# Windowed attention and a gated feed-forward in one kernel: products added in pairs on VectorE, q and k features taken at stride 4, three padded weight regions

## The chip, the cores and the metric

One Trainium2 chip, one of its cores. The metric is the time of one execution on the device, in microseconds (us).

## What is computed

One sequence of 2048 rows of width 512, in bf16. `xn` is the row-wise layer norm of `x`. Two branches read it:

```
qkv = xn @ wqkv                      # 32 heads of 16 features
logits[s, w] = q[s] . k[s - 2*w] / 4 # w = 0..7, one such row per head; masked where s - 2*w < 0
o = sum_w softmax(logits)[s, w] * v[s - 2*w]
s = o @ wo
g = silu((gelu(xn @ w_gate) * (xn @ w_up)) @ w_down)   # inner width 1792
out = x + s * g
```

So each query sees 8 keys, two rows apart, and the rest is dense matrix products.

## The kernel before

The sequence is cut into 4 blocks of 512 rows (index j). Everything is held with features on partitions and rows along the free dimension, so `xnT` comes from PE transposes (L355) of normalised tiles.

For each block there are these steps:

- **qkv** (L428): 12 groups of 4 matmuls give q, k and v in 4 chunks of 128 features each. A chunk's stationary operand is 128 neighbouring columns of `wqkv_sb`. For block 0 the groups work on halves of 256 rows, so that they can start on two tiles of `x`. ScalarE (ACT) copies each group out of PSUM (L441, L447, L452). v goes through DRAM (`vT_dram`) and comes back as `v_arr` with the window's shifts laid out on partitions (L494).
- **scores**: for `w2` = 0, 1 and each of 4 chunks VectorE (DVE) multiplies q by four shifted views of k into one product tile `prod` of 128x4x512 (L515). PE then sums over the 16 features of each head with a 0/1 matrix `ind`: 4 chunks times 4 shifts, 16 matmuls with 32 output columns each into one PSUM tile `L` (L528), the four shifts on four column strips. ACT takes the exponential (L540). For block 0 a small DVE instruction multiplies by a mask (L544).
- **normalisation**: PE sums the weights over w (L574), DVE takes the reciprocal (L584, L586), PE spreads it (L592), ACT copies it (L602), DVE multiplies (L612).
- **values**: for each half of the 16 features DVE makes four product tiles `pv` (L625), two feature groups times `w2` = 0, 1, and PE sums them over w with the matrix `fold4`, again 16 matmuls (L639); ACT copies `o` out (L650).
- **feed-forward**: 14 pairs of groups of 4 matmuls, `g` and `u` (L686); ACT takes the gelu (L696); DVE multiplies into `hT` (L703).
- **output**, 4 tiles of 128 rows: `y` (14 matmuls, L740), `s` (4 matmuls, L728), ACT's silu (L751), DVE's product and residual (L754, L761), the store (L765).

The order of instructions on every engine is fixed when the kernel is built. Class `Order` places tasks one after the other on modelled engines with durations such as `PROD = 1.14` and `COL16 = 1.1`; the dense matmuls form one chain on PE in the order qkv(0..3), then feed-forward and output of block 0, 1, 2, 3. Scores and values fill in by readiness and priority. A DVE product tile comes from a ring of 6 buffers (`pr`), the PSUM groups of the main chain from a ring of 4 (`f`), `L`, transposes, sums and spreads from a ring of 2 (`a`), `O` from 1.

The matrices are loaded by DMA. `load_wqkv` brings q, k and v columns in three pieces. ACT's queue issues the loads of `w_gate`, `w_up`, `wo` (four pieces) and `w_down`, each behind a step that it is told to wait for: `wo` behind the last k copy of block 2.

Nine matmuls on zeros of 512 columns (L293) run at the start, while `x` is on its way.

Of the kernel before, what the change touches and what calls it, by code (L numbers as in the profile page):

```python
# [19 lines left out]
TQ = 512  # L20
# [4 lines left out]

MM = 0.216
COL16 = 1.1
TR = 0.28
PROD = 1.14
HMUL = 0.6  # L30
# [99 lines left out]
def kernel(  # L130
# [11 lines left out]
    nc = tc.nc  # L142
    B, S, D = A_x.shape
    DF = B_w_gate.shape[1]
    NC = D // P
# [11 lines left out]
    cpool = pool("cpool", 1)  # L157
# [9 lines left out]
    hpool = pool("hpool", 1)  # L167
# [4 lines left out]
    psa = pool("psa", 2, space=bass.MemoryType.PSUM)  # L172
# [23 lines left out]

    def load_wqkv(i):
        nc.sync.dma_start(
            out=wqkv_sb[:, :, i * D : (i + 1) * D], in_=wqkv_v[:, :, i * D : (i + 1) * D]
        )  # L200

    def load_x(t0, t1):
# [24 lines left out]
    mhalf = cpool.tile([P, TPB], F32, name="mhalf")  # L227
    nc.gpsimd.memset(mhalf[:], -0.5)

    IOFF = 24  # L230
    ind = cpool.tile([P, 56], BF16, name="ind")
    nc.gpsimd.memset(ind[:], 0.0)
    nc.gpsimd.memset(ind[:, IOFF : IOFF + 8], 1.0)
    nc.gpsimd.affine_select(
        out=ind[:, IOFF : IOFF + 8],
        in_=ind[:, IOFF : IOFF + 8],
        pattern=[[-16, 8]],
        compare_op=ALU.is_ge,
        fill=0.0,
        base=0,  # L240
        channel_multiplier=1,
    )
    nc.gpsimd.affine_select(
        out=ind[:, IOFF : IOFF + 8],
        in_=ind[:, IOFF : IOFF + 8],
        pattern=[[16, 8]],
        compare_op=ALU.is_gt,
        fill=0.0,
        base=16,
        channel_multiplier=-1,  # L250
    )
    k_sb = cpool.tile([P, NC, PAD + S], BF16, name="k_sb")
# [35 lines left out]
    rstd = cpool.tile([P, NT, 1], F32, name="rstd")  # L288


    warm_ps = psa.tile([P, TQ], F32, name="warm_ps", tag="a")
    for _ in range(9):
        nc.tensor.matmul(warm_ps[:], lhsT=warm[:, 0:P], rhs=warm[:], start=True, stop=True)  # L293
    order.clock["pe"] = 5.0


# [3 lines left out]
    def layer_norm(j):  # L300
# [49 lines left out]
        def transpose(t, dep, on_act):  # L350
            def fn():
                tiles["tr", t] = psa.tile([P, NC * P], BF16, name="tr_ps", tag="a")
                for c in range(NC):
                    cs = slice(c * P, (c + 1) * P)
                    nc.tensor.transpose(tiles["tr", t][:, cs], tiles["xn", t][:, cs], ident[:])  # L355

            def copy():
                o = xnT[:, :, t * P : (t + 1) * P]
                i = tiles["tr", t][:].rearrange("p (c n) -> p c n", c=NC)
                if on_act:  # L360
                    nc.scalar.activation(out=o, in_=i, func=AF.Copy)
                else:
                    nc.vector.tensor_copy(out=o, in_=i)  # L363
# [48 lines left out]
    def qkv(j):  # L412
# [4 lines left out]
        for lo in range(0, TQ, n):  # L417
            for which in range(3):
                for c in range(0, NC, w):
                    key = (j, which, c, lo)  # L420

                    def mms(key=key, which=which, c=c, lo=lo):
                        ps = psf.tile([P, TQ], F32, name="qkv_ps", tag="f")
                        tiles["qkv", key] = ps
                        for i in range(w):
                            fo = which * NC + c + i
                            for dk in range(NC):
                                nc.tensor.matmul(  # L428
                                    ps[:, i * n : (i + 1) * n],
                                    lhsT=wqkv_sb[:, dk, fo * P : (fo + 1) * P],  # L430
                                    rhs=xnT[:, dk, j * TQ + lo : j * TQ + lo + n],
                                    start=(dk == 0),
                                    stop=(dk == NC - 1),
                                )
# [68 lines left out]
    def scores(j, prio):  # L503
        exps = []
        for w2 in range(2):
            prods = []

            def product(c, w2=w2, prods=prods):
                prod = prpool.tile([P, 4, TQ], BF16, name="prod", tag="pr")
                off = j * TQ + PAD - HALO + 8 * w2  # L510
                base = k_sb[:, c, off : off + TQ]
                kwin = bass.AP(
                    tensor=base.tensor, offset=base.offset, ap=[base.ap[0], [2, 4], [1, TQ]]
                )
                nc.vector.tensor_tensor(  # L515
                    out=prod[:],
                    in0=tiles["q", j][:, c, :].unsqueeze(1).to_broadcast([P, 4, TQ]),
                    in1=kwin,
                    op=ALU.mult,
                )  # L520
                prods.append(prod)

            def reduce(w2=w2, prods=prods):
                L = psa.tile([P, TQ], F32, name="L_ps", tag="a")
                tiles["L", j, w2] = L
                for cc in range(NC):
                    for w4 in range(4):
                        nc.tensor.matmul(  # L528
                            L[32 * w4 : 32 * (w4 + 1), :],
                            lhsT=ind[:, IOFF - 8 * cc : IOFF - 8 * cc + 32],  # L530
                            rhs=prods[cc][:, w4, :],
                            start=(cc == 0),
                            stop=(cc == NC - 1),
                        )

            def expo(w2=w2):
                if w2 == 0:
                    tiles["attn", j] = atpool.tile([P, 2, TQ], BF16, name="attn", tag="attn")
                attn = tiles["attn", j]
                nc.scalar.activation(out=attn[:, w2, :], in_=tiles["L", j, w2][:], func=AF.Exp)  # L540

            def masked(w2=w2):
                a = tiles["attn", j][:, w2, 0:PAD]
                nc.vector.tensor_tensor(out=a, in0=a, in1=mask[:, w2, :], op=ALU.mult)  # L544

            ps = []
            for c in range(NC):
                key = ("S", j, w2)
                ps.append(
                    add(  # L550
                        "dve", PROD, lambda c=c, product=product: product(c),
                        deps=[q_ready[j], k_ready[j], *ps[-1:]], prio=prio,
                        takes=[("pr", (*key, c))], opens=key, closes=key if c == NC - 1 else None,
                        frees=[("q", j)] if w2 == 1 and c == NC - 1 else [],
                    )
                )
            r = add(
                "pe", COL16, reduce, deps=[ps[-1]], prio=-0.5, takes=[("a", ("L", j, w2))],
                frees=[("pr", ("S", j, w2, c)) for c in range(NC)],
            )  # L560
# [48 lines left out]
    def values(j, prio):  # L609
# [10 lines left out]
        for half in range(2):  # L620
            pvs = []

            def product(g, w2, half=half, pvs=pvs):
# [6 lines left out]
                )  # L630
                pvs.append(pv)

            def reduce(half=half, pvs=pvs):
                o_ps = pso.tile([P, 2, TQ], F32, name="O_ps", tag="o")
                tiles["O", j, half] = o_ps
                for gg in range(2):
                    for ww in range(2):
                        for e in range(4):
                            nc.tensor.matmul(  # L639
                                o_ps[32 * e : 32 * (e + 1), gg, :],  # L640
                                lhsT=fold4[:, 0, :],
                                rhs=pvs[2 * gg + ww][:, e, :],
                                start=(ww == 0),
                                stop=(ww == 1),
                            )

            def evacuate(half=half):
                if half == 0:
# [8 lines left out]
            for i in range(4):  # L657
# [6 lines left out]
                        takes=[("pr", (*key, i))], opens=key, closes=key if last else None,  # L664
# [3 lines left out]
                )  # L668
            r = add(
                "pe", COL16, reduce, deps=[ps[-1]], prio=-0.5, takes=[("O", (j, half))],  # L670
                frees=[("pr", (*key, i)) for i in range(4)],
            )
            o_ready[j] = add(
                "act", ACT2, evacuate, deps=[r], prio=-0.6, frees=[("O", (j, half))],
# [208 lines left out]
```

## Time and profile before

| What | Value |
|---|---|
| time, median of 13 runs | 238.61 us (236.61 to 239.58) |
| the profiled execution: its own time | 238.75 us |
| its span, first to last instruction | 237.0 us |
| PE busy | 229.0 us, 97% |
| VectorE busy | 157.8 us, 67% |
| ScalarE busy | 109.8 us, 46% |
| GpSimd busy | 28.1 us, 12% |
| mean granted TensorE clock | 0.997 |

The thirteen times are 236.61, 236.97, 237.07, 237.12, 237.24, 237.25, 238.61, 238.62, 238.73, 238.75, 239.12, 239.33 and 239.58 us: six up to 237.25, seven from 238.61.

A duration in the trace runs from an instruction's start to its end, and neighbours on one engine overlap: what a row of equal instructions costs its engine is read from start to start. A line of the time line gives the start, the length of the merged stretch, and how many instructions are in it. PEld are the weight loads, which run beside the matmuls.

### The profile page before, as it was taken

The numbers are of one execution on the slowest core, as the hardware profiler recorded it, in microseconds if no ns is written. First come the engines' busy times: TensorE is split into PE (matmuls) and PEld (weight loads), VectorE is DVE, ScalarE is ACT, GpSimd is POOL, SyncE is SP. The second block draws the span as 40 slices with busy tenths as digits, with TensorE's granted clock in tenths as the row PEclk, the third lists the DMA queues.
The fourth block names the chain that finished last, engine by engine and source line by source line (L and its number), as shares of the span: only waits on it lengthen the run. The fifth ranks groups of instructions, "written<-read, shape, count | busy, mean of one in ns | idle before, by whom it ended". The sixth has DMA issues, their size and how long they took to land.

```text
span 237.0 us, 3474 instructions
## 1 busy us (share of the span) xinstructions
PE 229.0 (97%) x1334; PEld 106.6 (45%) x1357; DVE 157.8 (67%) x238; ACT 109.8 (46%) x166; POOL 28.1 (12%) x68
## 2 busy tenths in 40 slices
PE   7899999999999999999999999999999999999992
PEld 2696553443443443434444444444444444444441
DVE  4789998899999999999999321334332243433232
ACT  3466567475766345855532332463342244334211
POOL 7102920300333120003000000000000000000000
PEclk9999999999999999999999999999999999999998
DMA  6993799598497680007200001000000110000011
GB/s 185 358 364 118 159 209 366 141 296 282 130 192 163 126 183 0 22 26 178 46 0 3 0 0 44 22 25 0 1 3 0 44 44 0 3 0 1 22 35 32
DMA packets 15073, 22.66 MB, mean 96 GB/s; under 512 B 1472, under 2 KB 11984, under 8 KB 15056
## 3 DMA queue, kind: packets, MB, share of 16 engines
q0 software_dynamic: 2592, 8.54, 16.4%
q1 hardware_dynamic: 8592, 7.57, 10.2%
q10 hardware_dynamic: 3872, 6.32, 7.8%
q8 instruction: 10, 0.16, 0.3%
q14 instruction: 7, 0.06, 0.1%
HBM read 18.22 MB, written 4.21 MB: 95 GB/s over the span
## 4 chain that ended last, share of the span: by engine, by line
PE 83%; DMA 8%; DVE 6%; issue 1%; ACT 0%; ACTq 0%; DVEq 0%
PE g_ps L686 21%; PE y_ps L740 20%; PE u_ps L686 20%; PE qkv_ps L428 9%; DMA wu_sb<-in_B_w_up_dram 7%; PE s_ps L728 6%; PE O_ps L639 3%; DVE prod L515 3%; PE L_ps L528 2%; PE tr_ps L355 1%; DMA x_sb<-in_A_x_dram 1%; DVE rs L584 1%; DVE stats L307 1%; PE b_ps L592 0%; DVE sg L754 0%
## 5 line engine op out<-in xcount | busy, mean ns | idle before, releaser
L703 DVE TENSOR_TENSOR hT<-gl,u_ps 128x512 bf16<-128x512 bf16 x56 | 38.1, 683 | 33.5 <-PE u_ps L686 29.5
L696 ACT ACTIVATE gl<-g_ps 128x512 bf16<-128x512 f32 x56 | 33.2, 597 | 52.2 <-PE g_ps L686 47.7
L686 PE MATMUL g_ps<-xnT,wg_sb 128*128 128x512 bf16 x221 | 57.0, 379 | 0.2
L686 PE MATMUL u_ps<-xnT,wu_sb 128*128 128x512 bf16 x216 | 56.6, 379 | 0.4
L740 PE MATMUL y_ps<-wd_sb,hT 128*128 128x512 bf16 x218 | 50.7, 379 | 0.4
L428 PE MATMUL qkv_ps<-xnT,wqkv_sb 128*128 128x512 bf16 (+1 forms) x235 | 45.7, 345 | 0.9 <-DVE xnT L363 0.6
L515 DVE TENSOR_TENSOR prod<-q_sb,k_sb 128x2048 bf16<-128x2048 bf16 x32 | 37.7, 1218 | 1.0 <-PE L_ps L528 1.0
L625 DVE TENSOR_TENSOR pv<-attn,v_arr 128x2048 bf16<-128x2048 bf16 x32 | 37.9, 1216 | 0.0
L686 PEld LDWEIGHTS <-wg_sb 128*128 128x128 bf16 x224 | 21.7, 98 | 27.2 <-issue 1.6
L754 DVE TENSOR_TENSOR sg<-sil,s_ps 128x512 bf16<-128x512 bf16 (+2 forms) x17 | 11.1, 653 | 34.2 <-PE s_ps L728 22.9
L686 PEld LDWEIGHTS <-wu_sb 128*128 128x128 bf16 x224 | 21.5, 98 | 27.4 <-issue 2.1
L740 PEld LDWEIGHTS <-hT 128*128 128x128 bf16 x224 | 21.6, 98 | 26.1 <-issue 0.4
L428 PEld LDWEIGHTS <-wqkv_sb 128*128 128x128 bf16 x240 | 23.2, 101 | 18.5 <-issue 1.7
L751 ACT ACTIVATE sil<-y_ps 128x512 bf16<-128x512 f32 x16 | 9.6, 597 | 41.2 <-PE y_ps L740 41.2
L494 POOL DMA_DIRECT2D v_arr<-vT_dram x32 | 18.6, 589 | 65.5 <-DVE pv L625 50.3
L728 PE MATMUL s_ps<-wo_sb,o_sb 128*128 128x512 bf16 (+2 forms) x67 | 16.2, 366 | 0.0
L441 ACT ACTIVATE q_sb<-qkv_ps 128x512 bf16<-128x512 f32 x16 | 9.5, 601 | 6.0 <-PE qkv_ps L428 6.0
L307 DVE BATCH_NORM_STATS2 stats<-x_sb 128x6 f32<-128x512 bf16 x16 | 10.8, 672 | 2.0 <-DMA x_sb<-in_A_x_dram 2.0
L447 ACT ACTIVATE k_sb<-qkv_ps 128x512 bf16<-128x512 f32 x16 | 9.4, 597 | 5.2 <-PE qkv_ps L428 5.2
L452 ACT ACTIVATE vst<-qkv_ps 128x512 bf16<-128x512 f32 x16 | 9.2, 600 | 4.6 <-PE qkv_ps L428 4.6
L728 PEld LDWEIGHTS <-o_sb 128*128 128x128 bf16 x68 | 6.5, 98 | 7.3
L650 ACT ACTIVATE o_sb<-O_ps 128x1024 bf16<-128x1024 f32 x8 | 8.2, 1022 | 1.9 <-PE O_ps L639 1.4
(55 smaller groups left out, 113.9 us busy)
## 6 DMA issues: line engine op xcount, KB each, us to landing
v_arr<-vT_dram POOLq DMA_DIRECT2D x32, 260.0 KB, 5.2
vT_dram<-vst SPq DMA_DIRECT2D x16, 128.0 KB, 5.0
out_dram<-sg SPq DMA_DIRECT2D x15, 128.0 KB, 1.7
wg_sb<-in_B_w_gate_dram ACTq DMA_DIRECT2D x1, 1792.0 KB, 7.4
wu_sb<-in_B_w_up_dram ACTq DMA_DIRECT2D x1, 1792.0 KB, 15.7
wd_sb<-in_B_w_down_dram ACTq DMA_DIRECT2D x1, 1792.0 KB, 9.2
wqkv_sb<-in_A_wqkv_dram SPq DMA_DIRECT2D x3, 512.0 KB, 6.4
x_sb<-in_A_x_dram SPq DMA_DIRECT2D x2, 512.0 KB, 8.9
```

The costliest lines, as they stand in the source:

```text
L307: nc.vector.bn_stats(out=stats[:, t, :], in_=x_sb[:, t, :])
L428: nc.tensor.matmul(ps[:, i * n : (i + 1) * n], lhsT=wqkv_sb[:, dk, fo * P : (fo + 1) * P], rhs=xnT[:, dk, j * TQ + lo : j * TQ + lo + n], ...
L494: nc.gpsimd.dma_start(out=v_arr[32 * w4 : 32 * (w4 + 1), :, :], in_=src)
L515: nc.vector.tensor_tensor(out=prod[:], in0=tiles["q", j][:, c, :].unsqueeze(1).to_broadcast([P, 4, TQ]), in1=kwin, op=ALU.mult,)
L625: nc.vector.tensor_tensor(out=pv[:], in0=tiles["attn", j][:, w2, :].unsqueeze(1).to_broadcast([P, 4, TQ]), in1=tiles["va", j, half][:, 4 * ...
L686: nc.tensor.matmul(ps[:], lhsT=w[:, dk, fc * P : (fc + 1) * P], rhs=xnT[:, dk, j * TQ : (j + 1) * TQ], start=(dk == 0), stop=(dk == NC - 1),)
L696: nc.scalar.activation(out=tiles["gl", j, fc][:], in_=tiles["g_ps", j, fc][:], func=AF.Gelu_apprx_tanh)
L703: nc.vector.tensor_tensor(out=tiles["h", j][:, fc, :], in0=tiles["gl", j, fc][:], in1=tiles["u_ps", j, fc][:], op=ALU.mult,)
L728: nc.tensor.matmul(tiles["s", t][:, cs], lhsT=tiles["o", j][:, c, tt * P : (tt + 1) * P], rhs=wo_sb[:, c, cs], start=(c == 0), stop=(c == ...
L740: nc.tensor.matmul(tiles["y", t][:], lhsT=tiles["h", j][:, fc, tt * P : (tt + 1) * P], rhs=wd_sb[:, fc, :], start=(fc == 0), stop=(fc == N ...
L751: nc.scalar.activation(out=tiles["sil", t][:], in_=tiles["y", t][:], func=AF.Silu)
L754: nc.vector.tensor_tensor(out=tiles["sg", t][:, cs], in0=tiles["sil", t][:, cs], in1=tiles["s", t][:, cs], op=ALU.mult,)
```

## The change

Four things are changed together.

1. **Pairs.** After every second product tile DVE adds the two in place: for the scores chunks 0 and 1, then 2 and 3; for the values `w2` = 0 and 1 of one feature group, that is w and w + 4. PE then sums two tiles instead of four, with 8 matmuls instead of 16 (L and O alike). The second tile of a pair is free again after the addition.
2. **Features at stride 4.** So that chunks can be added before the sum over a head's features, chunk c of q and k now holds the features with d mod 4 = c: the stationary operand takes 128 columns at a step of 4 (from column c of the region). v is unchanged. The 0/1 matrix becomes `quad`: output column h sums partitions 4h to 4h + 3.
3. **Weight regions.** `wqkv_sb` is now three regions, q, k and v, each of 4 x 512 columns and 64 columns of padding. The three loads write the same bytes.
4. **Warm-up.** The PSUM tile of the nine zero matmuls comes from `O`'s pool, and two and three more of 256 columns follow the transposes of tile 0 and tile 1.

The planner's table gets `COL8 = 0.65` for the short sums; an addition is planned at `PROD`.

```diff
-                            lhsT=ind[:, IOFF - 8 * cc : IOFF - 8 * cc + 32],
-                            rhs=prods[cc][:, w4, :],
-                            start=(cc == 0),
-                            stop=(cc == NC - 1),
+                            lhsT=quad[:],
+                            rhs=prods[2 * i][:, w4, :],
+                            start=(i == 0),
+                            stop=(i == 1),
...
+            def pair(i, prods=prods):
+                a, b = prods[2 * i], prods[2 * i + 1]
+                nc.vector.tensor_tensor(out=a[:], in0=a[:], in1=b[:], op=ALU.add)
...
                 for gg in range(2):
-                    for ww in range(2):
-                        for e in range(4):
...
+                    for e in range(4):
+                        nc.tensor.matmul(
+                            o_ps[32 * e : 32 * (e + 1), gg, :],
+                            lhsT=fold4[:, 0, :],
+                            rhs=pvs[2 * gg][:, e, :],
+                            start=True,
+                            stop=True,
+                        )
...
+                                if which < 2:
+                                    ws = slice(dk * D + c + i, (dk + 1) * D, NC)
+                                else:
+                                    ws = slice(dk * D + (c + i) * P, dk * D + (c + i + 1) * P)
                                 nc.tensor.matmul(
                                     ps[:, i * n : (i + 1) * n],
-                                    lhsT=wqkv_sb[:, dk, fo * P : (fo + 1) * P],
+                                    lhsT=wqkv_sb[:, which, ws],
...
-    wqkv_sb = hpool.tile([P, NC, 3 * D], BF16, name="wqkv_sb", tag="h")
+    wqkv_sb = hpool.tile([P, 3, NC * D + 64], BF16, name="wqkv_sb", tag="h")
...
+                if t < 2:
+                    warm_up(2 + t, TQ // 2)
```

Since the planner places all tasks anew, other instructions move too. On VectorE, the stretch before the first value products, before (L515 are the score products, L612 the normalisation; `q_sb_426` is q of block 1, `q_sb_574` of block 2):

```order
L515 TENSOR_TENSOR prod_725<-q_sb_426,k_sb_142 128x2048
L515 TENSOR_TENSOR prod_748<-q_sb_426,k_sb_142 128x2048
L584 RECIPROCAL rs_770<-sum_ps_752 128x128
L586 CAST rs16_772<-rs_770 128x128
L515 TENSOR_TENSOR prod_786<-q_sb_426,k_sb_142 128x2048
L515 TENSOR_TENSOR prod_800<-q_sb_426,k_sb_142 128x2048
L515 TENSOR_TENSOR prod_810<-q_sb_574,k_sb_142 128x2048
L612 TENSOR_TENSOR attn_650<-attn_650,b_sb_802 128x1024
L515 TENSOR_TENSOR prod_837<-q_sb_574,k_sb_142 128x2048
L515 TENSOR_TENSOR prod_846<-q_sb_574,k_sb_142 128x2048
L584 RECIPROCAL rs_863<-sum_ps_848 128x128
L586 CAST rs16_865<-rs_863 128x128
```

and now (L517 are the score products, L527 the additions, L626 the normalisation; `q_sb_430` is q of block 1):

```order
L517 TENSOR_TENSOR prod_694<-q_sb_430,k_sb_141 128x2048
L517 TENSOR_TENSOR prod_715<-q_sb_430,k_sb_141 128x2048
L550 TENSOR_TENSOR attn_648<-attn_648,mask_158 128x16
L527 TENSOR_TENSOR prod_694<-prod_694,prod_715 128x2048
L598 RECIPROCAL rs_748<-sum_ps_730 128x128
L600 CAST rs16_750<-rs_748 128x128
L517 TENSOR_TENSOR prod_759<-q_sb_430,k_sb_141 128x2048
L517 TENSOR_TENSOR prod_773<-q_sb_430,k_sb_141 128x2048
L527 TENSOR_TENSOR prod_759<-prod_759,prod_773 128x2048
L626 TENSOR_TENSOR attn_648<-attn_648,b_sb_780 128x1024
L639 TENSOR_TENSOR pv_806<-attn_648,v_arr_475 128x2048
L639 TENSOR_TENSOR pv_816<-attn_648,v_arr_475 128x2048
```

Before, the scores of block 1 and half of those of block 2 stood ahead of the first value products: 20 score products and 6 value products come before the first `hT`. Now it is half of block 1's scores, 12 and 4 products and 8 additions, and one reciprocal in place of two; the rest stands behind, among the `hT`. On PE this makes 3 sums into `L` ahead of the first `g` instead of 5.

On ScalarE, while block 2's k and v are copied out, before (L447 copies k, L452 copies v, L540 is the exponential, of block 0 for `attn_650`):

```order
L447 ACTIVATE k_sb_142<-qkv_ps_661 128x512
L820 DMA wo_sb_109<-in_A_wo_dram 32x4x512 x4
L540 ACTIVATE attn_650<-L_ps_677 128x512
L452 ACTIVATE vst_720<-qkv_ps_670 128x512
L452 ACTIVATE vst_723<-qkv_ps_698 128x512
L452 ACTIVATE vst_745<-qkv_ps_706 128x512
L452 ACTIVATE vst_750<-qkv_ps_715 128x512
L540 ACTIVATE attn_767<-L_ps_727 128x512
L441 ACTIVATE q_sb_779<-qkv_ps_762 128x512
```

and now (L449, L454 and L546 in the same roles, `attn_648` of block 0):

```order
L449 ACTIVATE k_sb_141<-qkv_ps_656 128x512
L844 DMA wo_sb_109<-in_A_wo_dram 32x4x512 x4
L454 ACTIVATE vst_696<-qkv_ps_665 128x512
L454 ACTIVATE vst_707<-qkv_ps_672 128x512
L546 ACTIVATE attn_648<-L_ps_698 128x512
L454 ACTIVATE vst_724<-qkv_ps_680 128x512
L454 ACTIVATE vst_728<-qkv_ps_688 128x512
L443 ACTIVATE q_sb_745<-qkv_ps_710 128x512
```

The second exponential has moved behind two copies of v, and the third is gone from this place. On PE, 7 groups of qkv (the last three of k and four of v) now stand between the first and the second sum into `L`, where it was 4, and the next block's first q comes right behind the second sum.

More of the change, by code (lines that the diff above doesn't have):

```diff
@@ L243 @@
     nc.gpsimd.affine_select(
[L244 to L249, printed above, removed]
+        out=quad[:], in_=quad[:], pattern=[[4, 32]], compare_op=ALU.is_gt, fill=0.0, base=4,
         channel_multiplier=-1,
@@ L288, with warm_up @@
     rstd = cpool.tile([P, NT, 1], F32, name="rstd")
-    warm_ps = psa.tile([P, TQ], F32, name="warm_ps", tag="a")
-    for _ in range(9):
-        nc.tensor.matmul(warm_ps[:], lhsT=warm[:, 0:P], rhs=warm[:], start=True, stop=True)
+    warm_ps = pso.tile([P, 2, TQ], F32, name="warm_ps", tag="o")
+    def warm_up(count, n):
+        for _ in range(count):
+            nc.tensor.matmul(
+                warm_ps[:, 0, 0:n], lhsT=warm[:, 0:P], rhs=warm[:, 0:n], start=True, stop=True
+            )
+    warm_up(9, TQ)
     order.clock["pe"] = 5.0
@@ L525, in reduce @@
                 tiles["L", j, w2] = L
[L526 removed]
+                for i in range(2):
                     for w4 in range(4):
@@ L668, in values @@
                 )
+                if i % 2 == 1:
+                    ps.append(
+                        add(
+                            "dve", PROD, lambda i=i, pair=pair: pair(i // 2), deps=[ps[-1]], prio=prio,
+                            opens=key, closes=key if last else None, frees=[("pr", (*key, i))],
+                        )
+                    )
             r = add(
-                "pe", COL16, reduce, deps=[ps[-1]], prio=-0.5, takes=[("O", (j, half))],
-                frees=[("pr", (*key, i)) for i in range(4)],
+                "pe", COL8, reduce, deps=[ps[-1]], prio=-0.5, takes=[("O", (j, half))],
+                frees=[("pr", (*key, i)) for i in (0, 2)],
             )
```

50 lines of the change are left out of this document (25 added, 25 removed).

## The prediction

> **What bounds the kernel now.** I read the page's span and engine totals first, then the waits, then the windows of 60 to 130 us and behind it.
>
> ```profile
> span 237.0 us, 3474 instructions
> ...
> PE 229.0 (97%) x1334; PEld 106.6 (45%) x1357; DVE 157.8 (67%) x238; ACT 109.8 (46%) x166; POOL 28.1 (12%) x68
> ```
>
> ```profile
> PE qkv_ps L428 <- DVE xnT L363: 0.6, 1, 0.6
> ...
> PE b_ps L592 <- DVE rs L586: 0.3, 1, 0.3
> ```
>
> ```profile
> 60.00:130.00 70.00, 69.51 (x445) 29.31 (x453) 69.61 (x81) 39.88 (x52) 11.55 (x20) 1.00 0.40 88
> 130.00:237.00 107.00, 102.18 (x482) 46.41 (x489) 36.14 (x59) 34.52 (x51) 0.00 (x0) 0.99 0.05 15
> ```
>
> PE is busy nearly all the time, and once the real work has begun it waits twice for DVE, 0.9 us in all. So PE's queue sets the end. But DVE (the third pair in a window's row) is a second full engine up to 130 us: 69.61 of 70 us. Behind that it needs 36.14 of 107 us. So a microsecond off PE counts if DVE keeps up; and what DVE is given must spread into that later slack without PE reaching a result before DVE has made it.
>
> **Part 1, the shorter sums.** From start to start on PE:
>
> ```profile
> 37.05 1.05 PE L528 MATMUL L_ps<-prod,ind 128*32 128x512 bf16 x16
> 38.03 3.63 PE L428 MATMUL qkv_ps<-xnT,wqkv_sb 128*128 128x512 bf16 x15
> 41.59 1.05 PE L528 MATMUL L_ps<-prod,ind 128*32 128x512 bf16 x16
> ...
> 46.14 0.29 PE L574 MATMUL sum_ps<-attn,fold 128*32 128x128 bf16 x8
> 46.36 2.76 PE L428 MATMUL qkv_ps<-xnT,wqkv_sb 128*128 128x512 bf16 x11
> ```
>
> ```profile
> 108.02 1.05 PE L639 MATMUL O_ps<-pv,fold 128*32 128x512 bf16 x16
> 109.00 0.40 PE L592 MATMUL b_ps<-rs,spread 128*128 128x128 bf16 x4
> 109.23 1.03 PE L728 MATMUL s_ps<-wo_sb,o_sb 128*128 128x512 bf16 x4
> 110.09 0.81 PE L686 MATMUL g_ps<-xnT,wg_sb 128*128 128x512 bf16 x3
> ```
>
> Four full matmuls take 110.09 - 109.23 = 0.86 us, 0.216 each. A sum of 16 takes 0.98 us (38.03 - 37.05), and the 16 matmuls behind it 3.56 (one record is missing in the row) instead of 3.45: 1.09 in all. Sixteen strip matmuls, four abreast, are worth 16 x 0.216 / 4 = 0.86; the other 0.23 goes with the change of shape and stays. Halving takes 0.43 off each sum. There are 8 sums into L and 8 into O: 16 x 0.43 = **6.9 us less on PE**. Were the whole 0.98 in proportion, it would be 7.8: the upper end.
>
> **Part 2, the additions.**
>
> ```profile
> L515 DVE TENSOR_TENSOR prod<-q_sb,k_sb 128x2048 bf16<-128x2048 bf16 x32 | 37.7, 1218 | 1.0 <-PE L_ps L528 1.0
> ...
> L761 DVE TENSOR_TENSOR sg<-sg,x_sb 128x512 bf16<-128x512 bf16 x15 | 6.4, 425 | 0.5
> ```
>
> ```profile
> 59.78 4.62 DVE L625 TENSOR_TENSOR pv<-attn,v_arr 128x2048 bf16<-128x2048 bf16 x4
> 64.32 0.68 DVE L703 TENSOR_TENSOR hT<-gl,u_ps 128x512 bf16<-128x512 bf16 x1
> 64.92 1.22 DVE L625 TENSOR_TENSOR pv<-attn,v_arr 128x2048 bf16<-128x2048 bf16 x1
> ...
> 93.73 0.95 DVE L584 RECIPROCAL rs<-sum_ps 128x128 f32<-128x128 f32 x1
> ...
> 94.86 2.35 DVE L515 TENSOR_TENSOR prod<-q_sb,k_sb 128x2048 bf16<-128x2048 bf16 x2
> 97.13 0.68 DVE L754 TENSOR_TENSOR sg<-sil,s_ps 128x512 bf16<-128x512 bf16 x1
> 97.84 0.43 DVE L761 TENSOR_TENSOR sg<-sg,x_sb 128x512 bf16<-128x512 bf16 x1
> 98.18 0.68 DVE L612 TENSOR_TENSOR attn<-attn,b_sb 128x1024 bf16<-128x1024 bf16 x1
> 98.78 2.35 DVE L515 TENSOR_TENSOR prod<-q_sb,k_sb 128x2048 bf16<-128x2048 bf16 x2
> ```
>
> The residual (L761) is an in-place addition of bf16 tiles, 425 ns for 512 elements; a product takes 1218 for 2048. One line of 0.52 ns an element runs through both, so I give the addition, of the product's shape and kinds, the product's price. In a row that is (64.32 - 59.78) / 4 = 1.14 us. An instruction that reads what the one before it wrote starts after that one's end (L761 at 97.84, L754 ends at 97.81), while an independent one starts 0.09 before it (98.18 against 98.27): 0.12 more, 1.26 us. Thirty-two additions are **40 us more on DVE**, and they cost time only where PE comes to wait.
>
> Whether it does is a balance per block. DVE has now 16 products (18.2), 8 additions (10.1), 14 hT at 64.92 - 64.32 = 0.60 (8.4), four outputs at 98.18 - 97.13 = 1.05 (4.2), reciprocal and cast at 94.86 - 93.73 (1.13) and normalisation (0.60): 42.6 us. PE has 28 groups of 0.86 (24.2), 72 output matmuls (15.5), 4 sums of 0.43 + 0.23 (2.6), and sum over w and spread (0.6): 42.9 us. **The two are level**, and stay so through blocks 0, 1 and 2; only behind the last scores, at some 165 us, does DVE get slack. So it matters where DVE stands when the first block's feed-forward begins.
>
> ```profile
> 26.21 1.21 DVE L515 TENSOR_TENSOR prod<-q_sb,k_sb 128x2048 bf16<-128x2048 bf16 x1
> ...
> 45.48 0.17 DVE L544 TENSOR_TENSOR attn<-attn,mask 128x16 bf16<-128x16 bf16 x1 [0.99 <-ACT attn L540]
> ```
>
> ```profile
> 61.28 1.03 PE L686 MATMUL u_ps<-xnT,wu_sb 128*128 128x512 bf16 x4
> ```
>
> Before, 26 products, two reciprocals and 2.0 us of waits (the mask's 0.99, L515's 1.0 above) lie between 26.21 and the first hT at 64.32. Now it is 16 products, 8 additions and one reciprocal: 64.32 - 10 x 1.14 + 8 x 1.14 + 6 x 0.12 - 1.13 - 2.0 = 59.6. PE's first u ended at 61.28 + 0.86; five long sums ahead of it become three short ones (-5.5 + 2.0), one sum over w, one spread and the 0.3 of waiting go (-0.8): 57.8. DVE starts the first hT 1.8 us behind, and ends it 2.5 behind. Four PSUM banks let PE run three groups, 2.6 us, past a u whose hT is missing: just enough, with no margin. But PE is late for another reason:
>
> **Part 3, what the new order brings.**
>
> ```profile
> 28.50 15.71 DMA wu_sb<-in_B_w_up_dram
> ...
> 44.23 0.57 ACTq L820
> ...
> 44.85 0.61 ACT attn L540
> ```
>
> The last of wo's four loads is issued only when w_up has landed (28.50 + 15.71 = 44.21), and holds ACT's queue until 44.85. Queued behind it are now two copies of v ahead of the second exponential. PE leaves the first L at 37.05 + 0.54, does 28 matmuls (6.15) and the second L (0.54) by 44.3, with all four banks full of v. The next q needs a bank, and the first copy ends at 44.85 + 0.6. **PE waits 1.1 us** (0 if the loads go out sooner, 2 if PE comes sooner and w_up does not). The mask, behind copies and exponential, runs near 46.5. By DVE's own sum it would be 46.1 (45.48, less 2.0 of waits, 12 products become 10 and 4 additions): DVE loses 0.4 where PE loses 1.1, so the first hT is 1.1 instead of 1.8 behind, and there is a margin. I add 0.3 for small waits.
>
> **Part 4, strides and regions.** The weight loads now:
>
> ```profile
> L428 PEld LDWEIGHTS <-wqkv_sb 128*128 128x128 bf16 x240 | 23.2, 101 | 18.5 <-issue 1.7 <-DMA wqkv_sb<-in_A_wqkv_dram 0.8
> ```
>
> The b_ps row above has four loads and their matmuls in 0.23 us, so a contiguous load occupies at most 0.06, behind matmuls of 0.11 (256 columns, part 5) or 0.216. No row shows a strided load. At twice the price it is still hidden, so I take 0; the bounds are 0 and the +8.7 of rival 5. The three loads carry the same bytes: 0.
>
> [...]
>
> **Part 5, warm-up.**
>
> ```profile
> 1.25 4.02 PE L293 MATMUL warm_ps<-warm 128*128 128x512 bf16 x9 [1.25 <-DVE eps_sb L221]
> 5.41 1.13 PE L355 MATMUL tr_ps<-ident,xn_t 128*128 128x128 bf16 x8
> 7.14 4.32 PE L428 MATMUL qkv_ps<-xnT,wqkv_sb 128*128 128x256 bf16 x24 [0.61 <-DVE xnT L363]
> ...
> 12.62 2.78 PE L428 MATMUL qkv_ps<-xnT,wqkv_sb 128*128 128x256 bf16 x24
> ```
>
> ```profile
> 9.86 0.16 DVE L320 RECIPROCAL rstd<-rstd 128x1 f32<-128x1 f32 x1 [0.75 <-ACT rstd L314]
> ...
> 12.82 0.42 DVE L363 COPY xnT<-tr_ps 128x512 bf16<-128x512 bf16 x1 [0.74 <-PE tr_ps L355]
> ```
>
> The first 24 qkv matmuls took 4.32 us, the same 24 later 2.78: PE ran slowly at first, at half speed to go by the nine zero matmuls (4.02 / 9 = 0.45 against 0.216). If the five extra matmuls fill the hole between 5.3 and 7.1 so that PE is at full speed when qkv starts, 1.5 us go. DVE can follow: it stood 0.75 and 0.74 us in that stretch, behind these very matmuls. If they fail, the two between the transposes delay tile 1's by 0.3. The thirteen times of before lie in two groups some 1.7 us apart, and the profiled run is in the upper one: so the slow start may come and go already.
>
> The Trainium skill's "TensorE: Matmul & The Clock Gate" (Part 1) has a gate that opens after a free-running window of 3.4 us in which PE was busy. By it 4.0 us of zeros suffice only by luck, and a longer busy stretch more often.
>
> **The sum**, on the profiled execution's 238.75 us (1.75 above its span, 0.14 above the median of the 13): 238.75 - 6.9 + 1.1 + 0.3 = 233.25. With the warm-up at work 1.5 less, and 0.3 back because w_up need not land as much sooner as PE arrives: **232.0**. Without it, 0.3 more: 233.5.
>
> **The rivals.**
>
> ```profile
> L703 DVE TENSOR_TENSOR hT<-gl,u_ps 128x512 bf16<-128x512 bf16 x56 | 38.1, 683 | 33.5 <-PE u_ps L686 29.5 <-PE g_ps L686 2.1 <-ACT gl L696 1.8
> ```
>
> 1. *Forecast*: shorter sums and full speed from the start, 232.0. Chance 0.44.
> 2. *The slow start remains*: 233.5. For it: the hole is mostly transposes, and five short matmuls may not be enough. 0.33.
> 3. *DVE sets the pace.* If an addition takes 0.1 us more than a product, the 28 ahead of block 3's values put DVE 2.8 us behind, and 42.6 against 42.9 leaves no margin: 235 to 236. For it: two level engines, each now and then waiting for the other. Against: the residual shows no surcharge. 0.11.
> 4. *Additions at hT's rate* (683 ns for 512 where the residual takes 425, 1.03 us more for 2048): 28 x 1.03 = 29 us behind, 261, slower. It decides from a surcharge of 6.6 / 28 = 0.24 us on, where the gain on the median is gone. Against: L761 is all-bf16 in SBUF, as the additions are; hT reads PSUM. 0.04.
> 5. *Strided loads four times as long*, 0.23 us: 64 at 256 columns stick out by 0.115 (7.4), 96 at 512 by 0.014 (1.3): 240.7. 0.04.
> 6. *No gain*, as the sums are not on the path after all: 238.6. Against: PE's 0.9 us of waits. 0.04.
>
> **The numbers.** The likeliest case gives the time. The range takes in cases 1 and 2 and the nearer half of 3: from 229.8 (232.0 less part 1's further 0.9 and part 3's 1.1 plus 0.3, rounded) to 235.6. Left out are 4, 5, 6 and half of 3: 0.18. About 0.5%, 1.2 us, is what a measurement of this kernel can tell from no change. Faster (1 to 3): 0.88; the same (6): 0.04; slower (4 and 5): 0.08.
>
> **What would show it.** In the changed profile: PE busy near 222 us; a sum of 8 in 0.55 us from start to start; additions of 1.22 us; DVE full up to some 165 us, then nearly empty; a wait of PE for a bank near 45 us of about 1 us; q and k weight loads near 101 ns; the first 24 qkv matmuls in 2.8 us (case 1) or 4.3 (case 2). I am wrong if PE waits for hT or for the sums' inputs again and again between 60 and 165 us, if additions last over 1.3 us, or if the first 24 qkv are fast and the time is still above 233.5.

## The result and the profile after

The changed kernel takes 230.9 us in the median of 11 runs (230.51 to 232.31). A twelfth execution on record took 231.96 us; with it the median would be 231.06. The kernel before takes 238.61 in the median of 48 (236.29 to 240.49), the thirteen above included. The ratio is 0.9707, with a 95% interval from 0.9678 to 0.9735. The profiled execution took 232.29 us, with a span of 230.6, and so is one of the slower ones of the eleven: six of them took 230.51 to 230.9. Four executions of the kernels below, of 304.1, 471.57, 471.97 and 823.08 us, lasted far longer than all others of the same kernel (in the two profiled ones, 471.57 and 471.97, PE was at half speed from end to end, and the first 24 qkv matmuls took 5.60 and 5.72 us); with one of 234.5 us in experiment 3, 1.6% above the fastest of its kernel, they are left out of every number that follows.

The page's span, engine totals and DVE's row of the time line (40 slices, busy share in tenths):

```profile
span 230.6 us, 3251 instructions
...
PE 220.4 (96%) x1213; PEld 104.9 (45%) x1234; DVE 193.4 (84%) x270; ACT 111.1 (48%) x167; POOL 27.9 (12%) x67
...
DVE  4799999899999999999999999999849997333222
```

PE has lost 8.6 us of work and DVE has got 35.6 more. DVE is full up to slice 29, some 167 us, once more for three slices behind 173 (block 3's values), and needs a third or less of the last six. The windows ahead of and behind the last scores (PE first, DVE third) say it in microseconds:

```profile
60.00:166.00 106.00, 105.16 (x557) 45.40 (x565) 104.64 (x123) 50.18 (x70) 10.73 (x19) 1.00 0.27 61
166.00:230.60 64.60, 59.66 (x302) 26.75 (x300) 35.13 (x50) 23.75 (x33) 0.00 (x0) 1.00 0.05 17
```

For 106 us both engines run without a gap worth the name: two full engines side by side, where before it was so up to 130 us. Now the groups of the sums and of the additions, and the list of PE's waits (total, times, longest, in us):

```profile
L649 DVE TENSOR_TENSOR pv<-pv 128x2048 bf16<-128x2048 bf16 x16 | 19.5, 1219 | 0.2
L527 DVE TENSOR_TENSOR prod<-prod 128x2048 bf16<-128x2048 bf16 x16 | 19.5, 1219 | 0.2
L534 PE MATMUL L_ps<-prod,quad 128*32 128x512 bf16 x64 | 4.9, 384 | 0.0
L656 PE MATMUL O_ps<-pv,fold 128*32 128x512 bf16 x64 | 4.9, 384 | 0.0
```

```profile
PE qkv_ps L430 <- ACT vst L454: 1.7, 1, 1.7
PE warm_ps L285 <- DVE eps_sb L223: 1.2, 1, 1.2
PE qkv_ps L430 <- DVE mv L304: 1.0, 1, 1.0
```

An addition lasts 1219 ns, as long as a product. The list has no wait of PE for a sum's input, a reciprocal or `hT`; once the real work has begun, what PE waits for is one copy of v. That place on PE's time line (start, length, count; in brackets the idle time ahead) and on ACT's, where ACTq rows are the issuing of DMAs:

```profile
36.44 0.61 PE L534 MATMUL L_ps<-prod,quad 128*32 128x512 bf16 x8
36.99 6.24 PE L430 MATMUL qkv_ps<-xnT,wqkv_sb 128*128 128x512 bf16 x27
43.15 0.62 PE L534 MATMUL L_ps<-prod,quad 128*32 128x512 bf16 x8
45.43 1.89 PE L430 MATMUL qkv_ps<-xnT,wqkv_sb 128*128 128x512 bf16 x8 [1.67 <-ACT vst L454]
```

```profile
40.50 4.16 ACTq L844 DMA_DIRECT2D wo_sb<-in_A_wo_dram  x3
44.78 1.09 ACT L454 ACTIVATE vst<-qkv_ps 128x512 bf16<-128x512 f32 x2 [4.26 <-DMA wu_sb<-in_B_w_up_dram]
```

A sum of 8 takes 36.99 - 36.44 = 0.55 us from start to start, where one of 16 took 0.98. Three issues of `wo` hold ACT's queue for 4.16 us, since the last of them goes out only at 44.09, when `w_up` has landed (27.89 + 16.18 = 44.07; in the trace the two loads share one completion semaphore); the copies of v behind them free the banks, and PE stands 1.67 us. At the start of the program:

```profile
8.04 2.81 PE L430 MATMUL qkv_ps<-xnT,wqkv_sb 128*128 128x256 bf16 x24 [0.98 <-DVE mv L304]
```

```profile
8.03 1.02 PEld L430 LDWEIGHTS <-wqkv_sb 128*128 128x128 bf16 x10 [1.26 <-DMA wqkv_sb<-in_A_wqkv_dram]
```

The first 24 qkv matmuls take 2.81 us instead of 4.32, but start at 8.04 instead of 7.14. The list of PE's waits names DVE's `mv`, which had long been done; the weight loads' row shows the true cause, the q weights, which landed late in this execution.

The two spans differ by 6.4 us. From the rows: 16 sums at 0.98 - 0.55 = 0.43 are 6.9 less; the first qkv matmuls 1.5 less; their later start 0.9 more; the bank wait 1.67 more; the 0.3 that PE waited for a reciprocal is gone. That is 6.1 less, and 0.3 us are left over.

### The profile page after: what moved, and what is told of

The parts are those of the page before. It is cut to its first block, busy times and chain, and to the rows that moved or that the text cites. A ratio compares the mean times of both kernels' runs of the same rounds, so it can differ in the third digit from the quotient of the medians.

```text
span 230.6 us, 3251 instructions
## 1 busy us (share of the span) xinstructions
PE 220.4 (96%) x1213; PEld 104.9 (45%) x1234; DVE 193.4 (84%) x270; ACT 111.1 (48%) x167; POOL 27.9 (12%) x67
## 4 chain that ended last, share of the span: by engine, by line
PE 87%; DMA 8%; DVE 2%; issue 1%; ACT 1%; ACTq 0%; DVEq 0%
PE u_ps L710 21%; PE g_ps L710 21%; PE y_ps L764 21%; PE qkv_ps L430 12%; DMA wu_sb<-in_B_w_up_dram 7%; PE s_ps L752 6%; PE O_ps L656 2%; PE L_ps L534 1%; PE tr_ps L351 1%; DMA x_sb<-in_A_x_dram 1%; DVE stats L303 1%; ACT vst L454 1%; PE sum_ps L588 0%; PE b_ps L606 0%; DVE sg L778 0%
## 5 line engine op out<-in xcount | busy, mean ns | idle before, releaser
L430 PE MATMUL qkv_ps<-xnT,wqkv_sb 128*128 128x512 bf16 (+1 forms) x235 | 43.5, 336 | 2.9 <-ACT vst L454 1.7
L639 DVE TENSOR_TENSOR pv<-attn,v_arr 128x2048 bf16<-128x2048 bf16 x32 | 38.4, 1218 | 0.1
L517 DVE TENSOR_TENSOR prod<-q_sb,k_sb 128x2048 bf16<-128x2048 bf16 x32 | 38.3, 1216 | 0.0
L430 PEld LDWEIGHTS <-wqkv_sb 128*128 128x128 bf16 x240 | 24.9, 108 | 18.0 <-issue 2.5
L649 DVE TENSOR_TENSOR pv<-pv 128x2048 bf16<-128x2048 bf16 x16 | 19.5, 1219 | 0.2
L527 DVE TENSOR_TENSOR prod<-prod 128x2048 bf16<-128x2048 bf16 x16 | 19.5, 1219 | 0.2
L454 ACT ACTIVATE vst<-qkv_ps 128x512 bf16<-128x512 f32 x16 | 9.4, 600 | 7.5 <-DMA wu_sb<-in_B_w_up_dram 4.3
L449 ACT ACTIVATE k_sb<-qkv_ps 128x512 bf16<-128x512 f32 x16 | 9.2, 597 | 3.9 <-PE qkv_ps L430 3.9
```

The lines of the kernel that those rows point to most:

```text
L430: nc.tensor.matmul(ps[:, i * n : (i + 1) * n], lhsT=wqkv_sb[:, which, ws], rhs=xnT[:, dk, j * TQ + lo : j * TQ + lo + n], start=(dk == 0), ...
L517: nc.vector.tensor_tensor(out=prod[:], in0=tiles["q", j][:, c, :].unsqueeze(1).to_broadcast([P, 4, TQ]), in1=kwin, op=ALU.mult,)
L527: nc.vector.tensor_tensor(out=a[:], in0=a[:], in1=b[:], op=ALU.add)
L639: nc.vector.tensor_tensor(out=pv[:], in0=tiles["attn", j][:, w2, :].unsqueeze(1).to_broadcast([P, 4, TQ]), in1=tiles["va", j, half][:, 4 * ...
L649: nc.vector.tensor_tensor(out=a[:], in0=a[:], in1=b[:], op=ALU.add)
```

## The experiments

**1. The sums alone.** The additions stay, but each added tile is read twice, so that PE has its 16 matmuls back (the sum over O in the same way):

```diff
-                for i in range(2):
+                for i in range(4):
...
-                            rhs=prods[2 * i][:, w4, :],
+                            rhs=prods[2 * (i // 2)][:, w4, :],
...
-                            stop=(i == 1),
+                            stop=(i == 3),
...
```

> The changed kernel, but each sum into L and into O is again 16 matmuls, with every added tile read twice (so the sums are doubled, and the output is not the reference's). The additions and the order on VectorE and ScalarE stay. If the sums lie on the path at the size of part 1, PE gets 16 x 0.43 = 6.9 us back: 237.8 us. If their whole length is in proportion, 7.8: 238.7. If PE had hidden room behind VectorE, so that the gain came from something else (the new order, the warm-up), less than 2 us: below 233.

Measured: 237.26 us in the median of 12 runs (236.82 to 238.12), 6.4 above the changed kernel. The groups of the sums, and PE's place of the bank wait:

```profile
L657 PE MATMUL O_ps<-pv,fold 128*32 128x512 bf16 x128 | 8.4, 382 | 0.0
L534 PE MATMUL L_ps<-prod,quad 128*32 128x512 bf16 x128 | 8.4, 382 | 0.0
```

```profile
36.66 1.05 PE L534 MATMUL L_ps<-prod,quad 128*32 128x512 bf16 x16
37.63 6.23 PE L430 MATMUL qkv_ps<-xnT,wqkv_sb 128*128 128x512 bf16 x27
43.80 1.05 PE L534 MATMUL L_ps<-prod,quad 128*32 128x512 bf16 x16
44.80 1.68 PE L430 MATMUL qkv_ps<-xnT,wqkv_sb 128*128 128x512 bf16 x7
```

Both groups are back at 8.4 from 4.9, 7.0 us in all, and the sum is back at 37.63 - 36.66 = 0.97. The wait for a bank is gone, since PE comes later to it; that is why the time rises by less than the 7.0, to 237.26 and not to the expected 237.8. The shorter sums are the bulk of the gain, at the forecast size, and the rival "no gain" is refuted.

**2. The warm-up alone.** The kernel before, with nothing but the five short zero matmuls and the other PSUM tile for them:

```diff
+                if t < 2:
+                    warm_up(2 + t, TQ // 2)
```

> The kernel before with only the warm-up of the change (the zero matmuls' PSUM tile from O's pool, two and three short ones behind the first two transposes). If they bring PE to full speed: 24 matmuls in 2.8 us, the upper group of before's times vanishes, median 236.8 to 237.4 against 238.6, so some 1.5 us of the 7.7 gained come from here and some 6.2 from the rest. If not: 238.6, two groups as before.

Measured: 237.34 us in the median, 236.83 to 238.23 in 11 runs; ratio to the kernel before 0.9938 (0.9908 to 0.9967), 1.5 us. The upper one of the two groups of times is gone. In its profile:

```profile
1.25 4.02 PE L295 MATMUL warm_ps<-warm 128*128 128x512 bf16 x9 [1.25 <-DVE eps_sb L221]
...
7.69 2.79 PE L436 MATMUL qkv_ps<-xnT,wqkv_sb 128*128 128x256 bf16 x24 [0.47 <-DMA wqkv_sb<-in_A_wqkv_dram]
```

The same nine zeros in the same 4.02 us as before, and then 24 matmuls in 2.79 instead of 4.32. Experiment 1's 6.4 and this 1.5 make 7.9, where the whole change gained 7.7: beside the bank wait, nothing of size is left for the new order or the padded regions. The regions were not tried alone.

**3. Everything but the warm-up**, twice:

```diff
-                if t < 2:
-                    warm_up(2 + t, TQ // 2)
```

> The changed kernel without the five short zero matmuls behind the first transposes (the nine long ones stay). If these five bring PE to full speed before the first qkv matmul: the first 24 of 256 columns take about 4.3 us again instead of 2.8, or do so in part of the executions, and the median rises from 230.9 by 0.8 to 1.6 us, to 231.7 to 232.5. If the fast start in the changed kernel's profile was chance: within 0.4 us of 230.9.

> The changed kernel without the five short zero matmuls, once more, for a profile of an execution in which PE is not slow throughout. If the five matmuls are what lets PE start at full speed, the first 24 qkv matmuls take about 4.3 us and the time is 1.3 to 1.8 above the changed kernel's 230.9, some 232.5; if the nine zero matmuls are enough by themselves, 2.8 us and 230.9.

Measured: 230.8, 231.56, 232.55 and 233.84 us in a first series of runs, 230.82, 231.05, 232.22 and 233.19 us in a second. The median of the eight, 231.89, is 1.0 above 230.9. The profile of the second series is of its 230.82:

```profile
1.25 4.02 PE L285 MATMUL warm_ps<-warm 128*128 128x512 bf16 x9 [1.25 <-DVE eps_sb L223]
5.76 0.99 PE L351 MATMUL tr_ps<-ident,xn_t 128*128 128x128 bf16 x8 [0.49 <-DVE xn_t L335]
7.36 2.78 PE L428 MATMUL qkv_ps<-xnT,wqkv_sb 128*128 128x256 bf16 x24 [0.61 <-DVE xnT L359]
```

Here PE was at full speed at 7.36 without any help, after the same 4.02 us of zeros after which it was slow in the kernel before. The clock records kept in the traces (from when on which share of the TensorE clock was granted; ahead of the first record the pages print full speed) say the same: full speed is granted from 6.24 us on here, and from 10.32 us in the kernel before, where the first qkv weight loads start 0.213 us apart up to 10.30 and 0.109 us apart from there on. In the nine profiles with the five extra matmuls it is granted between 3.94 and 6.82 us, each time ahead of the first qkv matmul. So the nine zeros suffice in some executions and not in others. With the five extra matmuls the times end at 232.31 (17 runs of the changed kernel, the six of experiment 5 included); without them three of eight are above that. So the warm-up appears to buy its 1.5 us in a part of the executions; the slower executions without it have no profile, so that they began at half speed is not shown. The profile of the second series gives the second of the two answers that stood in its expectation, and its slower times fit the first: there is no one time without the warm-up.

**4. Stride 4 undone.** q and k take neighbouring columns again, from the padded regions; the features are then not those that the sums need, so the output is not the reference's, and the work is the same:

```diff
-                                if which < 2:
-                                    ws = slice(dk * D + c + i, (dk + 1) * D, NC)
-                                else:
-                                    ws = slice(dk * D + (c + i) * P, dk * D + (c + i + 1) * P)
+                                ws = slice(dk * D + (c + i) * P, dk * D + (c + i + 1) * P)
```

> The changed kernel with q's and k's stationary operands taken from 128 neighbouring columns again, so that the pairs add products of other heads' features and the output is not the reference's; all else as in the changed kernel. If the stride costs nothing, as forecast: weight loads back from 113 to 98 ns at the median, time within 0.3 us of 230.9. If the longer loads reach the path (64 of them stand before matmuls of 256 columns): 0.5 to 1 us faster, 229.9 to 230.4, with the first 24 qkv matmuls below 2.8 us.

Measured: 230.96 us in the median of 6 (230.34 to 232.19), no difference. The 240 weight loads of the changed kernel, two thirds of which are those of q and k, and then of this one (minimum, median and maximum in ns, first and last start):

```profile
L430 PEld LDWEIGHTS <-wqkv_sb x240: 96/113/133, 8.0 to 56.6; 128*128 128x128 bf16 x120
```

```profile
L427 PEld LDWEIGHTS <-wqkv_sb x240: 95/98/99, 7.7 to 55.2; 128*128 128x128 bf16 x120
```

With stride 4 the median load lasts 113 ns, without it 98, and the time does not show it: the loads lie beside matmuls of 0.11 and 0.216 us.

**5. The bank wait taken away.** The fourth issue of `wo`, the one that stood until `w_up` had landed, goes to GpSimd's queue; the compute instructions keep their order:

```diff
-            start(wo_sb[32 * e : 32 * (e + 1), :, :], v[e], k_ready[2])
+            start(
+                wo_sb[32 * e : 32 * (e + 1), :, :], v[e], k_ready[2],
+                nc.gpsimd if e == 3 else nc.scalar,
+            )
```

> The changed kernel with the fourth of wo's loads issued by GpSimd's queue, so that ScalarE's queue is not held until w_up has landed; order of all compute instructions unchanged. If PE's wait of 1.7 us for a PSUM bank near 45 us is on the path: the wait goes, and 1.0 to 1.6 us with it, 229.3 to 229.9. If DVE is next in line (level with PE per block, and some 2 us behind it at the first hT): waits of PE for hT or sums of 0.5 us and more appear between 55 and 165 us, and at most 0.5 us is gained, 230.4 or more.

> The changed kernel as it is, beside the two that follow, so that they are compared on one chip: 230.9 us again, with PE's wait for a PSUM bank near 45 us between 0.7 and 1.7 us in the profile.

> The changed kernel with the issue of wo's fourth load moved from ScalarE's queue to GpSimd's, once more. If the bank wait near 45 us (0.7 to 1.7 us in three profiles) is on the path, 0.5 to 1.0 us below the changed kernel's time of this call; if the first run's 230.4 against 230.9 came from another chip or hour, no difference.

Measured: 230.37 us in the median of 6 (230.3 to 230.81) in the first series; in the second 230.67 (230.27 to 232.81) beside 230.99 (230.47 to 231.8) of the changed kernel itself. The first q behind the second sum on PE, and ACT, in the profile of the first series:

```profile
43.05 1.92 PE L430 MATMUL qkv_ps<-xnT,wqkv_sb 128*128 128x512 bf16 x8
```

```profile
39.86 1.26 ACTq L844 DMA_DIRECT2D wo_sb<-in_A_wo_dram  x2
41.24 1.08 ACT L454 ACTIVATE vst<-qkv_ps 128x512 bf16<-128x512 f32 x2 [1.37 <-PE qkv_ps L430]
```

and the changed kernel's in the second series, in an execution whose qkv began at the same 7.41 us:

```profile
44.33 1.89 PE L430 MATMUL qkv_ps<-xnT,wqkv_sb 128*128 128x512 bf16 x8 [1.21 <-ACT vst L454]
```

Two issues instead of three, ACT stands for PE and not the other way round, and the next q starts at 43.05 instead of 44.33. The lead reaches the end: the last store is issued at 225.43 instead of 226.62 us, 1.19 earlier, and the spans of these two executions, 228.6 and 229.5, differ by 0.9. On the medians it is 0.5 and 0.3, less than the 1.0 to 1.6 and the 0.5 to 1.0 that I had expected; the wait itself, between 0.7 and 1.7 us, and the start of qkv move from one execution to another. The waits of PE for `hT` or sums that the first expectation named as the other case are in neither profile. So the issue of `wo` is the cause of the wait, as the prediction has it. This is the fastest version tried, but six runs against six barely tell 0.3 us apart.

**6. DVE slowed down.** If DVE is level with PE, whatever is added to the additions must come out at the end. First a little: each addition in four pieces (both kinds alike).

```diff
-                nc.vector.tensor_tensor(out=a[:], in0=a[:], in1=b[:], op=ALU.add)
+                for g4 in range(4):
+                    nc.vector.tensor_tensor(
+                        out=a[:, g4, :], in0=a[:, g4, :], in1=b[:, g4, :], op=ALU.add
+                    )
```

> The changed kernel, with each addition cut into four pieces of 128x512. By the residual's 425 ns and the 0.09 that neighbours overlap, four pieces take 4 x 0.335 = 1.34 us where one addition takes 1.14 in a row: 0.20 us more each, a little under the 0.24 from which rival 4 called the gain gone. If VectorE is as full as PE up to 165 us (the balance of 42.6 against 42.9 per block), the 28 additions ahead of block 3's values cost 28 x 0.20 = 5.6 us less some 1 us of margin: 235 to 236. If VectorE still had slack there, at most 1 us: below 232.

> Additions in four pieces once more, for a profile of an execution in which PE has its full speed: 235 to 235.5 us, VectorE busy throughout from 60 to 170 us, and PE waiting for its tiles (the sums' inputs, hT, the reciprocal) some 3 to 4 us in all. If PE's waits are not there but its matmuls last longer, the loss is elsewhere than in VectorE's pace.

Measured: 235.42, 234.66, 237.49 and 235.29 us in the first series, 235.43 in the median of 4 (234.86 to 235.98) in the second, 4.4 above the changed kernel's 230.99 in that series. On DVE and PE, near one of the sums:

```profile
80.38 1.44 DVE L528 TENSOR_TENSOR prod<-prod 128x512 bf16<-128x512 bf16 x4
81.72 0.70 DVE L733 TENSOR_TENSOR hT<-gl,u_ps 128x512 bf16<-128x512 bf16 x1
```

```profile
81.17 1.08 PE L537 MATMUL L_ps<-prod,quad 128*32 128x512 bf16 x8
82.18 1.04 PE L716 MATMUL u_ps<-xnT,wu_sb 128*128 128x512 bf16 x4
...
92.99 0.61 PE L537 MATMUL L_ps<-prod,quad 128*32 128x512 bf16 x8
93.54 1.68 PE L770 MATMUL y_ps<-wd_sb,hT 128*128 128x512 bf16 x7
```

```profile
L537 PE MATMUL L_ps<-prod,quad 128*32 128x512 bf16 x64 | 7.1, 384 | 0.0
L662 PE MATMUL O_ps<-pv,fold 128*32 128x512 bf16 x64 | 7.1, 384 | 0.0
```

Four pieces take 81.72 - 80.38 = 1.34 us. PE reaches the sum at 81.17 while the second pair is still being added, and does its matmuls at the rate of the pieces: 1.01 us to the next group instead of 0.55. The sums' groups grow from 4.9 to 7.1 each, 4.4 us in all, as much as the medians differ. In the two profiled executions of that series the spans, 233.2 and 229.5, differ by 3.7, since the bank wait is 0.39 us here and 1.21 there. None of the loss stands in the list of PE's waits: the pieces follow each other every 0.335 us, less than a matmul's 384 ns from start to modelled end, so that the gaps pass for work. I had expected 3 to 4 us of listed waits; the time was right, the place (the sums, and neither `hT` nor the reciprocal) is narrower than I had put it. By its letter the second case of that expectation came, no waits and longer groups; but only the groups that read the additions grew, and one matmul lasts 384 ns as before, so it is DVE's pace all the same.

Then a lot: a second addition behind each, into the freed tile.

```diff
                 nc.vector.tensor_tensor(out=a[:], in0=a[:], in1=b[:], op=ALU.add)
+                nc.vector.tensor_tensor(out=b[:], in0=a[:], in1=b[:], op=ALU.add)
```

> The changed kernel, with a second addition behind each, into the tile that has just become free and that nothing reads (the output stays). The price of an addition is doubled: 1.26 us more each, and 28 of them stand ahead of block 3's values. If VectorE is level with PE: 28 x 1.26 = 35 us, less 1 us of margin, 263 to 266. If the path were PE's alone with VectorE's waits as room, clearly less, 250 or below.

Measured: 266.96 us in the median of 4 (265.19 to 267.17), 36 above the changed kernel, a little above the upper end. PE's list of waits:

```profile
PE O_ps L658 <- DVE pv L650: 9.7, 6, 2.6
PE L_ps L535 <- DVE prod L527: 7.2, 6, 2.4
PE b_ps L607 <- DVE rs L601: 4.1, 3, 2.3
```

Here the waits are long enough to be listed. Doubling the additions costs all that it adds to the 28 (28 x 1.26 = 35.3) and 0.7 us more, where some room should have come off: DVE had next to no room left. Whether the excess comes from the stretches in which PE itself was slow (last section) stays open.

## Why the prediction was right

The time, 230.9, is 1.1 below the 232.0 of the forecast, and the likeliest case is the one that came.

- **What bounds the kernel.** PE and a DVE that is full beside it: confirmed from both sides, by 6.4 us more when PE gets its matmuls back and by 4.4 and 36 us more when DVE gets longer additions.
- **Part 1, 6.9 us.** A sum of 8 takes 0.55 from start to start, to the hundredth. The 28 qkv matmuls behind it take 43.15 - 36.99 = 6.16, 0.11 above 28 x 0.216: the change of shape stays, as said. The groups' 7.0 us and the 6.4 of the time agree, the rest being the bank wait that goes again.
- **Part 2, additions at the product's price.** 1219 against 1218 ns; rivals 3 and 4 fell with that. Mis-sized was the 0.12 that a dependent instruction waits: where an addition follows something else than its own product, as 22 of the 32 do, it takes 102.35 - 101.22 = 1.13 (below), so DVE's busy time rose by 35.6 us and not by 40. The balance per block holds all the same: DVE full up to 166 us, PE not waiting for it. The four pieces measure the margin: 28 x (1.34 - 1.13) = 5.9 us were added and 4.4 arrived, so some 1.5 us of room were left. Rival 4's point, 0.24 us more per addition, was put somewhat low: at 0.21, 4.4 of the 7.7 us that the change gained were gone, and with 1.5 of room the rest would be gone at (7.7 + 1.5) / 28 = 0.33.

```profile
101.22 1.22 DVE L649 TENSOR_TENSOR pv<-pv 128x2048 bf16<-128x2048 bf16 x1
102.35 1.22 DVE L639 TENSOR_TENSOR pv<-attn,v_arr 128x2048 bf16<-128x2048 bf16 x1
```

- **Part 3, the bank wait.** Right in place and cause; 1.67 in the profiled execution, 1.2 in the next and 0.7 with contiguous loads, where the forecast was 1.1 (and 0.3 more with PE early). Its price on the medians of experiment 5 was less, 0.3 to 0.5. The 0.3 set aside for small waits was not needed: behind 60 us no wait of PE for DVE or ACT is listed, and the 0.3 that PE waited for a reciprocal, which the sum had not taken off, is gone. These terms, 1.7 us in the sum, were too large: by 1.2 to 1.4 if the medians are taken, by 0.5 if the 1.2 us of the profile in experiment 5 is, which with the reciprocal's 0.3 makes 0.8. Which of the two makes up the 1.1 us between forecast and result, no run settles. The later start of qkv (part 5), which the sum left out, went the other way and hides a part of the error; to that extent the closeness of the two times is luck.
- **Part 4, strides at 0.** Right on the time. On the loads themselves, "near 101 ns" was wrong for the strided ones, whose median is 113. The Trainium skill, "SBUF — State Buffer" (Door 1), has strides of up to 8 bf16 elements as free; on a load the records show 15% more, and on the time nothing.
- **Part 5, the warm-up.** Right, 1.5 us by its rows and by experiment 2's ratio. That "the slow start may come and go already" agrees with experiment 3, where it is absent from the one profile without the warm-up. The Trainium skill's "TensorE: Matmul & The Clock Gate" (Part 1) has a free-running window; it agrees, in that 4.02 us of the same zeros were enough at 230.82 us and not at 238.75. What the prediction left out is that the landing of the q weights moves from execution to execution: in the profiled execution qkv waited for them until 8.04 and gave 0.9 of the 1.5 back. In the changed kernel's second profile it started at 7.41, behind the copies of `xnT` and not behind the weights, and gave back 0.27; the prediction had put 0.3 on the delay of these transposes, but only for the case that the warm-up fails.

## What to carry to other kernels

Weigh the work that moves between two full engines as a balance per block, and ask at which surcharge per instruction it tips; here 0.2 us on each of 28 additions took more than half of the gain. A sum on PE that is fed piece by piece hides its waits in its own busy time, so compare its group's busy time, not only the list of waits. When a change brings instructions ahead of a queue's DMA issue, look at what that issue waits for, and try it on a queue where nothing urgent stands behind it.

## What was not expected of the hardware

In the kernel with doubled additions PE ran slowly after one wait and not after another of the same length:

```profile
132.23 0.40 PE L658 MATMUL O_ps<-pv,fold 128*32 128x512 bf16 x4 [2.38 <-DVE pv L650]
132.56 1.38 PE L712 MATMUL u_ps<-xnT,wu_sb 128*128 128x512 bf16 x3
133.73 1.91 PE L712 MATMUL g_ps<-xnT,wg_sb 128*128 128x512 bf16 x4
135.44 1.57 PE L712 MATMUL u_ps<-xnT,wu_sb 128*128 128x512 bf16 x4
136.84 1.03 PE L712 MATMUL g_ps<-xnT,wg_sb 128*128 128x512 bf16 x4
```

Behind 2.38 us of standing still, three groups of 4 matmuls (one record is missing in the first) took 136.84 - 132.56 = 4.28 us, where three groups otherwise take 2.6. Another wait of the same length left the speed as it was, 94.57 - 93.70 = 0.87 for the next group:

```profile
93.37 0.40 PE L535 MATMUL L_ps<-prod,quad 128*32 128x512 bf16 x4 [2.38 <-DVE prod L527]
93.70 1.04 PE L712 MATMUL u_ps<-xnT,wu_sb 128*128 128x512 bf16 x4
94.57 1.03 PE L754 MATMUL s_ps<-wo_sb,o_sb 128*128 128x512 bf16 x4
```

The granted TensorE clock (in these rows of 10 us each the third number from the end) was full around the second wait and not around the first:

```profile
90.00:100.00 10.00, 7.46 (x47) 3.11 (x46) 9.93 (x11) 4.36 (x5) 0.00 (x0) 1.00 0.00 0
130.00:140.00 10.00, 7.72 (x30) 3.15 (x31) 9.93 (x12) 2.73 (x5) 2.32 (x4) 0.83 0.50 107
```

The trace's clock records place it: half speed was granted from 133.12 to 136.53, that is for 3.41 us, and likewise from 68.26, 170.66 and 197.97 us on. In the order of time these four starts lie 19, 11 and 8 times 3.41 us apart, on one even grid. In the 3.41 us ahead of each of them PE was busy for only 0.85, 0.97, 1.12 and 1.11 us; up to 259 us every other stretch of that grid has at least 1.8. The wait that left the speed as it was falls into two stretches, 88.75 to 92.16 and 92.16 to 95.57, with 2.22 and 2.20 us of work. So in this execution it is a stretch of the grid with little work, and not the length of one wait, that goes ahead of half speed. Only this one profile shows it, and no run shifts a wait to test it.

PE's busy time rose from 220.4 to 231.8 us for the same matmuls. Whether that adds to the 36 us of this kernel, or passes unseen while PE is behind DVE anyway, no run tells apart.
